# Batch 1 in aligned key sets, one-operation activations for two batches, and other places for the copies of the global values

## The chip, the cores and the metric

The kernel runs on one core of one Trainium2 chip. The metric is the device time of one execution in microseconds. Before the change it is 296.8 us, the median of three runs (296.14 to 297.85).

## The reference, cut to what matters

```python
B, H, Sl, Sg, D = 8, 8, 512, 32, 64          # batches, heads, local and global rows, head size
k_all = concat(k_g, k_l); v_all = concat(v_g, v_l)
out_g = softmax(q_g @ k_all.T / 8) @ v_all   # 32 global rows see all 544 keys
s_ll = q_l @ k_l.T / 8, only where |i - j| <= 32
s_lg = q_l @ k_g.T / 8                       # and all 32 global keys
out_l = softmax(concat(s_lg, s_ll)) @ concat(v_g, v_l)
x = concat(out_g, out_l), heads side by side # 4352 rows of 512
h = x @ w_in                                 # 512 -> 2048
out = (h * sigmoid(1.702 h)) @ w_out         # 2048 -> 512
```

Inputs and output are float32; the kernel multiplies in bf16.

## The kernel before

The work goes batch by batch (i from 0 to 7, and a ninth block of the 256 global rows of all batches). For each there are three kinds of work:

- Attention, in two halves of four heads, `a` and `c` (in each half a head has 32 of the 128 partitions). `Tk` and `Tq` turn keys and queries on VectorE, `ext` puts the global ones beside them, `S(0)` and `S(1)` make the scores on TensorE, `X` the exponentials on ScalarE, `M` multiplies by the mask on VectorE, `U` or `UG` multiplies by the values on TensorE, and `R`, `XL`, `G` or `RXG` divide by the sums on VectorE and write xL (the batch's input of the next stage) and xG (the global rows).
- The hidden stage, `h_mm` and `h_act`: 16 steps of four matmuls of 512 columns, each with tanh on ScalarE and a multiply-add on VectorE (L656), since h * sigmoid(1.702 h) is half of h * (1 + tanh(0.851 h)). The result is `gT`; the half is put into the copy at the end (`o_out`, L687, scale 0.5).
- The output stage, `o_mm`: four blocks of 128 rows (`tci`), each of four groups (`f4`) of four matmuls, then a copy to `ob` on ScalarE and four writes by SP (L698).

The order on every engine is the program's order, written out by hand. The attention of batch i + 1 is laid between the output matmuls of batch i. Below, h0, o0, h1, o1, h2 are the hidden and the output stages of batches 0, 1 and 2. From batch 2 on all batches have one form, class `Wide`: keys in sets of 96 with the 32 global keys beside them (so that one matmul of 128 rows covers both), the values in three copies that start at different keys. `load_v` reads the values and, five times, the global values into `vtiles` (two, used in turn), and `turn_v`, on SP's queue, writes the shifted copies `vturn` in SBUF, in the middle of a hidden stage. Batches 0 and 1 have the older form, class `Quad`: four overlapping windows of keys, global keys apart (`gk`, `K`, `XK`, `ekU`), a shifted copy `ek2` of the global part for half of batch 1 by DMA, and `U` with the values as weights.

PSUM has eight banks of 512 columns: four in two pairs (`spair`, for scores, or for the first four hidden steps of batch 0), and four in the ring `psP` (`pbank`) that hidden, output and value products take in turn. A matmul that starts in a bank waits until the bank's last reader is done. GpSimd issues the loads (each issue also waits for the transfer eight before it) and makes the masks. `after(x)` is a small copy on GpSimd that reads x, and so holds back the loads that stand behind it.

Of the kernel before, what the change touches and what calls it, by code (L numbers as in the profile page):

```python
# [12 lines left out]
F32 = mybir.dt.float32  # L13
# [7 lines left out]
def kernel(  # L21
# [67 lines left out]
    def load_v(b):  # L89
        vt = v_rows(b)  # L90
        if b < 4:
            nc.gpsimd.memset(vt[:, :, :, D:], 1.0)
        vs, vg = (x[b].rearrange("h s d -> s h d") for x in (v_l, v_g))
        for c in range(5):
            nc.gpsimd.dma_start(out=vt[0:96, c, :, :D], in_=vs[96 * c : 96 * c + 96])  # L95
            nc.gpsimd.dma_start(out=vt[96:128, c, :, :D], in_=vg)  # L96
        nc.gpsimd.dma_start(out=vt[0:32, 5, :, :D], in_=vs[480:512])

# [11 lines left out]
    rvg = consts.tile([128, 4, D + 2], BF16)  # L110


    rvt = consts.tile([128, 4, D + 2], BF16)
# [5 lines left out]
    def load_g(lo, hi, names="kqv"):  # L119
        for name, dst, src in (("k", rkg, kgf), ("q", rqg, qgf)):  # L120
            if name in names:
                nc.gpsimd.dma_start(out=dst[:, lo:hi, :], in_=src[:, lo:hi, :])
        if "v" in names:
            load_turned(nc.gpsimd, rvg[:, lo:hi, :D], vgf[:, lo:hi, :])
# [33 lines left out]
    for i in range(2):  # L158
        vtiles.append(consts.tile([128, 8 * 6 * (D + 2)], BF16, name="v%d" % i))
        nc.gpsimd.memset(v_view(i, 4)[:, :, :, :, D:], 1.0)  # L160
# [25 lines left out]
    keep(28, psP.tile([128, 512], F32, name="w", tag="p"), 128)  # L186

    qtiles = []
    for i in range(4):
        qt = consts.tile([128, 24, 32], F32, name="q%d" % i)  # L190
        nc.vector.memset(qt[:, 0:4, :], 0.0)
        nc.vector.memset(qt[:, 20:24, :], 0.0)
        qtiles.append(qt)

    WIN = ((0, 10), (6, 12), (14, 12), (22, 10))
    near_mask = consts.tile([128, 2, LW], BF16)
# [15 lines left out]
    def make_near(c):  # L212
        nr = WIN[c][1]
        at = (0, 160, 0, 192)[c]
        nc.scalar.activation(near_mask[:, c // 2, at : at + 16 * nr].rearrange("p (t r) -> p t r", t=16),
                             near(bandt, c), AF.Copy)

# [5 lines left out]
    def mask_put(g, first, last, by, late):  # L223
# [22 lines left out]
    qgT = consts.tile([128, 4, 40], F32)  # L246
    nc.vector.memset(qgT[:, :, 32:], 0.0)
    kgT = consts.tile([128, 4, 32], F32)
# [12 lines left out]
    def load_rest():  # L261
        load_v2(0)
# [5 lines left out]
        for g4 in (1, 0, 2, 3):  # L268
            nc.gpsimd.dma_start(
                out=w_out_sb[:, 4 * g4 : 4 * g4 + 4, :].rearrange("p (g e) m -> p g (e m)", e=2),  # L270
                in_=w_out_r[:, 2 * g4 : 2 * g4 + 2, :])
            if g4 == 0:
                load(1, (0,))
                load_g(2, 4)
        load(1, (1,))
        load(2, kq=False)
        nc.gpsimd.dma_start(out=loaded[2][1][:, 0], in_=qf[2][:, 0])
        load_g(4, 8, "k")
        load_v2(1)
        load_g(4, 8, "q")  # L280
        nc.gpsimd.dma_start(out=loaded[2][0], in_=kf[2])
        nc.gpsimd.dma_start(out=loaded[2][1][:, 1], in_=qf[2][:, 1])
# [14 lines left out]
    class Quad:  # L297
        def __init__(self, Q):
# [5 lines left out]
            self.v = v_view(self.b, 4 if self.b < 2 else 5)[:, self.u]  # L304
            if self.b < 2:
# [43 lines left out]
        def S(self, rnd, split=False, added=False, part=None):  # L349
# [19 lines left out]
            if not part:  # L369
                self.E[rnd] = att.tile([128, 4, RW + 32], BF16, name="e%d" % rnd)  # L370
# [29 lines left out]
        def M(self, rnd):  # L400
            at = 36 if rnd else 40
            e = self.E[rnd][:, :, at : at + LW]
            nc.vector.tensor_mul(e, e, near_mask[:, rnd : rnd + 1, :].to_broadcast([128, 4, LW]))

# [25 lines left out]
        def XK(self, two=True):  # L430
            self.ek = att.tile([128, Sl], BF16, name="ek")
            nc.scalar.activation(self.ek, self.kb, AF.Exp, scale=scale)
            self.ek2 = None
            if two:
                self.ek2 = att.tile([128, Sl], BF16, name="ek2")
                load_turned(nc.sync, self.ek2, self.ek)

        def ekU(self, unit, warm=0, ov=None):
# [4 lines left out]
            for j in range(4):  # L443
                two = unit == 1 and self.ek2 is not None
                r = 32 * ((j + 1 + two) % 4)
                p = slice(r, r + 32)
                lv = (ones32[p] if unit == 0 else
                      (rvt if two else rvg)[p, self.Q, :D].rearrange("p (w h) -> p w h", h=2)[:, :, unit - 1])
                nc.tensor.matmul(ov[32 * j : 32 * j + 32, :], lhsT=lv, rhs=(self.ek2 if two else self.ek)[p],  # L449
                                 start=True, stop=False, skip_group_check=True)  # L450

        def ekUs(self, nxt=None, rnd=0, banks=(None, None, None)):
# [5 lines left out]
            if self.ek2 is not None:  # L458
                self.ekU(1, ov=banks[1])
            if nxt:  # L460
                nxt.K(1)
            if self.ek2 is None:
                self.ekU(1, ov=banks[1])
# [76 lines left out]
    class Wide(Quad):  # L540
# [9 lines left out]
        def spread(self):  # L550
# [3 lines left out]
            nc.scalar.activation(self.kg4[:, :, 0:96], kl[:, 0:480].rearrange("p (m w) -> p m w", m=5), AF.Copy)  # L554
            nc.scalar.activation(self.kT[:, 640:672], kl[:, 480:512], AF.Copy)
# [15 lines left out]
        def S(self, rnd):  # L571
# [14 lines left out]
            self.E[rnd] = att.tile([128, 4, LW], BF16, name="e%d" % rnd)  # L586
# [13 lines left out]
        def UG(self):  # L600
            self.ov = []
            for lo, hi in self.BANKS:
                ov = pbank("ov")
                self.ov.append(ov)
                work = []
                for t in range(lo, hi):
                    w = min(max(t, 1), 14)
                    work.append((t // 8, t + 1 if t < 8 else t - 8, w, 128, t - lo))
                if hi == 16:
                    work += [(*g, 4) for g in OUTER]  # L610
                for i, (rnd, o, w, n, to) in enumerate(work):
                    rho, m = at_of(w)
# [6 lines left out]
        def RXG(self):  # L619
            rc = att.tile([128, 17, 1], F32, name="rc")  # L620
# [17 lines left out]

    gTs, ops = {}, {}
# [12 lines left out]
    def h_act(i, fc, hp):  # L652
        n = width(i)
        th = moe.tile([128, TB], F32, name="th", bufs=4)
# [23 lines left out]
    def o_out(i, tci, op):  # L678
        ob = moe.tile([128, d_model], F32, name="ob", bufs=6)
        last = i == B and tci == B // 4 - 1  # L680
        for lo, hi in ((0, 320), (320, 512)) if last else ((0, 512),):
# [5 lines left out]
            nc.scalar.activation(ob[:, lo:hi], op[:, lo:hi], AF.Copy, scale=0.5)  # L687
            for j in range(4):
                eng = nc.scalar if last and j % 2 else nc.sync
                if 2 <= i < B:  # L690
# [8 lines left out]

    def act4(i, hf):  # L700
        f = slice(2 * hf, 2 * hf + 2)
        nc.vector.scalar_tensor_tensor(gTs[i][:, f, :], in0=th4s[i][:, f], scalar=1.0, in1=pts[i][hf],
                                       op0=ALU.add, op1=ALU.mult)

    pts, th4s = {}, {}
# [39 lines left out]
    a.XK(False)  # L745
# [5 lines left out]
    c.XK(False)  # L751
# [12 lines left out]
    pt = pts[0] = spair()  # L764
# [17 lines left out]
    th4 = th4s[0] = early  # L782

    def tanh2(hf):
        f = slice(2 * hf, 2 * hf + 2)
        nc.scalar.activation(th4[:, f], pt[hf], AF.Tanh, scale=0.851)

    tanh2(0)
    c.G()
    act4(0, 0)  # L790
    for fc in range(4, FC):
        h_step(0, fc)
        if fc in (5, 6, 8, 9):
            make_near((5, 6, 8, 9).index(fc))
        if fc == 12:
            tanh2(1)
            act4(0, 1)
    load_v(2)
# [7 lines left out]
    load_turned(nc.sync, rvt[:, 2:4], rvg[:, 2:4])  # L806
    nq = {1: (Quad(2), Quad(3)), 2: (Wide(4), Wide(5))}
    a, c = nq[1]
    a.T()
    transpose_g(2, 4)  # L810
    a.ext()
    osteps(0, (0, 1), (0, 0), (1, 1), (1, 0), (2, 1))
    a.S(0)
    a.gg()
    a.K()
    a.X(0)
    a.XK()
    a.M(0)
    a.eg()
    c.T()  # L820
    c.ext()
    osteps(0, (2, 0), (0, 2), (0, 3))
    a.S(1)
    a.X(1)
    a.M(1)
    osteps(0, (1, 2), (1, 3))
    c.S(0)
    c.X(0)
    c.M(0)
    osteps(0, (2, 2), (2, 3))  # L830
    c.S(1)
    a.ekUs(c, 1)
    c.X(1, lambda: c.XK(False))
    for unit in range(3):
        a.U(unit)
    a.R()
    nq[2][0].Tq()
    c.M(1)
    c.eg()
    pt = spair()  # L840
    a.Gm(bank(pt, 0)[:, 0 : D + 2])
    osteps(0, (3, 0), (3, 1))
    a.XL(0)
    a.XL(1)
    c.ekUs(banks=[bank(pt, unit + 1) for unit in range(3)])
    for unit in range(3):
        c.U(unit)
    c.R()
    c.XL(0)
    c.XL(1)  # L850
    a.G()
    c.Gm()
    osteps(0, (3, 2), (3, 3))
    a, c = nq[2]
    gTs[1] = moe.tile([128, FC, TB], BF16, name="gT")

    def loads(i):
        if i + 2 < B:
            after(gTs[i][:, 0])
            load(i + 2)  # L860
            if i == 1:
                load_g(8, NQ, "kq")
            load_v(i + 2)

    hps = [pbank("hp") for _ in range(2)]
    for fc, kcs in ((0, (0, 1)), (1, (0, 1)), (0, (2, 3)), (1, (2, 3))):
        h_mm(1, fc, hps[fc], kcs)
    for fc in range(FC):
        if fc < 2:
            h_act(1, fc, hps[fc])  # L870
        else:
            h_step(1, fc)
        if fc == 0:
            loads(1)
        if fc == 1:
            nq[1][1].G()
        if fc == 2:
            a.Tk()
        if fc == 5:
            a.spread()  # L880
        if fc == 7:
            a.ext()
        if fc == 8:
            turn_v(2)
        if fc == 10:
            a.S(0)
            a.X(0)
    a.M(0)

    def phase_o(i):  # L890
# [11 lines left out]
        if i == 1:  # L902
            c.Tk()
        a.S(1)
        a.X(1)
        if i == 1:
            c.spread()
        a.M(1)
        if i == 1:
            c.Tq()  # L910
            c.ext()
# [97 lines left out]
```

## Time and profile before

| | |
|---|---|
| profiled execution | 297.65 us, of which the span (first to last instruction) is 295.9 |
| median of three runs | 296.8 us |
| TensorE busy | 282.7 us (96%) |
| VectorE, ScalarE, GpSimd busy | 200.7, 161.4, 84.4 us |
| hidden matmuls L648 | 487 recorded, 108.3 us |
| output matmuls L673 | 486 recorded, 119.1 us |
| chain that ended last | PE 86%, DMA 5%, DVE 3%, issue 2%, ACT 2% |

The chain follows the work back from the last instruction, at each step to what released it. "Idle before" is the time in which an engine stood before an instruction, with what ended it. Times in the answers of the trace are microseconds from the start of the span.

### The profile page before, as it was taken

To read this page: it belongs to the slowest core of one execution; us is meant where nothing else is said; L and a number is where in the kernel's file an instruction comes from. 1 tells how busy PE (TensorE), PEld (TensorE's weight loads), DVE (VectorE), ACT (ScalarE), POOL (GpSimd) and SP (SyncE) were. 2 spreads that over 40 slices of the span, in tenths; PEclk is the share of its full clock that TensorE was granted. 3 is DMA by queue.
4 is the path that set the end of the run, shared out by engine and by line. 5 is a ranking of instruction groups with operands and counts; after the bars stand their busy time and mean duration, and the time that the engine had idled before them with its cause. 6 is when DMAs were issued, how large, how long until landed. Compare 5 with 4: busy or idle time off the path is not lost.

```text
span 295.9 us, 9591 instructions
## 1 busy us (share of the span) xinstructions
PE 282.7 (96%) x4076; PEld 145.0 (49%) x4129; DVE 200.7 (68%) x409; ACT 161.4 (55%) x282; POOL 84.4 (29%) x151
## 2 busy tenths in 40 slices
PE   7799999999999999999999999999999999999994
PEld 6354434444554455445454445444544454456553
DVE  6587956997968876777767767787678654773310
ACT  4727567277546645566547734764556551763421
POOL 6853556584504240162107130353000000000000
PEclk9999999999999999999999999999999999999999
DMA  7999999989934992299527992399226012101123
GB/s 196 153 177 210 194 190 212 169 155 210 139 76 115 229 104 67 72 188 193 80 55 153 222 102 55 82 235 151 65 59 181 2 47 65 38 0 35 39 62 80
DMA packets 63418, 35.94 MB, mean 121 GB/s; under 512 B 49808, under 2 KB 52240, under 8 KB 63376
## 3 DMA queue, kind: packets, MB, share of 16 engines
q0 software_dynamic: 53296, 17.77, 56.1%
q1 hardware_dynamic: 9328, 16.85, 20.4%
q10 hardware_dynamic: 752, 0.72, 0.8%
q8 instruction: 32, 0.52, 0.8%
q14 instruction: 10, 0.08, 0.1%
HBM read 36.70 MB, written 8.91 MB: 154 GB/s over the span
## 4 chain that ended last, share of the span: by engine, by line
PE 86%; DMA 5%; DVE 3%; issue 2%; ACT 2%; ACTq 0%; POOL 0%; SPq 0%; DVEq 0%
PE hp L648 38%; PE op L673 35%; PE s L581 5%; PE ov L614 4%; DMA ek<-ek 2%; DMA rk<-in_k_l_dram 2%; PE s L648 1%; ACT e L396 1%; DMA early<-in_k_l_dram 1%; DVE xL L508 1%; PE ov L475 1%; PE op L685 1%; PE s L363 1%; PE ov L449 0%; DVE rs L503 0%
## 5 line engine op out<-in xcount | busy, mean ns | idle before, releaser
L673 PE MATMUL op<-w_out_sb,gT 128*128 128x512 bf16 x486 | 119.1, 380 | 3.5 <-issue 2.1
L656 DVE SCALAR_TENSOR_TENSOR gT<-th,hp 128x512 bf16<-128x512 f32 (+1 forms) x140 | 90.3, 655 | 35.3 <-ACT th L655 34.3
L648 PE MATMUL hp<-xL,w_in_sb 128*128 128x512 bf16 x487 | 108.3, 379 | 0.9 <-DVE xL L508 0.2
L655 ACT ACTIVATE th<-hp 128x512 f32<-128x512 f32 (+1 forms) x140 | 79.1, 572 | 43.2 <-PE hp L648 42.9
L648 PEld LDWEIGHTS <-w_in_sb 128*128 128x128 bf16 x576 | 56.1, 98 | 64.9 <-issue 1.1
L673 PEld LDWEIGHTS <-gT 128*128 128x128 bf16 x528 | 48.3, 98 | 52.4 <-issue 1.4
L590 ACT ACTIVATE e<-s 128x704 bf16<-128x704 f32 x48 | 33.7, 755 | 24.5 <-PE s L581 24.5
L687 ACT ACTIVATE ob<-op 128x512 f32<-128x512 f32 (+2 forms) x35 | 20.5, 585 | 46.2 <-PE op L673 39.8
L596 DVE TENSOR_TENSOR e<-e,mask 128x1024 bf16<-128x1024 bf16 (+1 forms) x24 | 17.4, 724 | 22.4 <-ACT e L590 22.4
L95 POOL DMA_DIRECT2D v<-in_v_l_dram x30 | 23.6, 786 | 23.5 <-PE hp L648 14.1
L96 POOL DMA_DIRECT2D v<-in_v_g_dram x30 | 17.7, 590 | 18.3 <-DMA rk<-in_k_l_dram 14.9
L628 DVE TENSOR_TENSOR xn<-ov,rc 128x384 bf16<-128x384 f32 (+1 forms) x36 | 19.5, 542 | 1.2
L168 POOL CAST tick<-gT 1x1 f32<-1x1 bf16 x5 | 0.9, 174 | 59.8 <-DVE gT L656 59.8
L581 PEld LDWEIGHTS <-kT 32*128 32x128 bf16 x1344 | 12.4, 92 | 10.2 <-issue 9.3
L396 ACT ACTIVATE e<-s 128x856 bf16<-128x856 f32 x14 | 11.7, 881 | 7.3 <-PE s L363 7.3
L581 PE MATMUL s<-q,kT 32*128 32x32 bf16 (+2 forms) x1344 | 15.2, 184 | 0.0
L627 DVE RECIPROCAL rc<-ov 128x6 f32<-128x6 f32 (+1 forms) x36 | 6.6, 183 | 9.8 <-PE ov L614 9.8
L614 PEld LDWEIGHTS <-e 128*32 128x32 bf16 (+1 forms) x1056 | 10.1, 94 | 5.1 <-DVE kl L547 2.1
L547 DVE STREAM_TRANSPOSE kl<-rk 128x512 f32<-128x512 f32 x12 | 12.4, 1034 | 0.1
L560 DVE STREAM_TRANSPOSE q<-rq 128x512 f32<-128x512 f32 x12 | 12.5, 1039 | 0.0
L614 PE MATMUL ov<-v,e 128*32 128x66 bf16 (+1 forms) x528 | 11.0, 197 | 0.0
L614 PE MATMUL ov<-vt,e 128*32 128x66 bf16 x528 | 10.4, 195 | 0.0
(110 smaller groups left out, 187.6 us busy)
## 6 DMA issues: line engine op xcount, KB each, us to landing
out_dram<-ob SPq DMA_DIRECT2D x132, 64.0 KB, 2.0
vt<-v SPq DMA_DIRECT2D x12, 264.0 KB, 8.7
rk<-in_k_l_dram POOLq DMA_DIRECT2D x6, 512.0 KB, 11.7
vt<-v SPq DMA_DIRECT2D x6, 495.0 KB, 5.0
v<-in_v_l_dram POOLq DMA_DIRECT2D x30, 96.0 KB, 9.3
rq<-in_q_l_dram POOLq DMA_DIRECT2D x5, 512.0 KB, 8.3
w_in_sb<-in_moe_w_in_dram POOLq DMA_DIRECT2D x8, 256.0 KB, 9.0
w_out_sb<-in_moe_w_out_dram POOLq DMA_DIRECT2D x4, 512.0 KB, 10.5
```

The lines of the kernel that those rows point to most:

```text
L95: nc.gpsimd.dma_start(out=vt[0:96, c, :, :D], in_=vs[96 * c : 96 * c + 96])
L96: nc.gpsimd.dma_start(out=vt[96:128, c, :, :D], in_=vg)
L581: nc.tensor.matmul(bank(self.ps, j)[:, 0:LW].rearrange("p (t q) -> p t q", q=32)[:, os], lhsT=self.k[p, k0 : k0 + 128, e], rhs=self.q[p, t ...
L590: nc.scalar.activation(self.E[rnd][:, 2 * i : 2 * i + 2, :], self.ps[i][:, :, :LW], AF.Exp, scale=scale)
L596: nc.vector.tensor_mul(e, e, m.to_broadcast([128, 4, n]))
L614: nc.tensor.matmul(ov[32 * j : 32 * j + 32, 66 * to : 66 * to + 66], lhsT=self.E[rnd][0:n, j, 32 * o : 32 * o + 32], rhs=self.vs[rho][0:n, ...
L628: nc.vector.tensor_mul(xn[:, lo // 2 : hi // 2].rearrange("p a h w b -> p a b h w"), o3[:, 0:n, 0:D].rearrange("p (a b) (w h) -> p a b h w ...
L648: nc.tensor.matmul(hp[:, : width(i)], lhsT=w_in_c[:, fc // 4, kc, fc % 4 // 2, :, fc % 2], rhs=(xL[i] if i < B else xG)[:, kc, :], start=( ...
L655: nc.scalar.activation(th[:, :n], hp[:, :n], AF.Tanh, scale=0.851)
L656: nc.vector.scalar_tensor_tensor(gTs[i][:, fc, :n], in0=th[:, :n], scalar=1.0, in1=hp[:, :n], op0=ALU.add, op1=ALU.mult)
L673: nc.tensor.matmul(op, lhsT=gTs[i][:, fc, tci * 128 : tci * 128 + 128], rhs=w_out_sb[:, fc, :], start=(first and fc == 4 * f4), stop=(fc = ...
L687: nc.scalar.activation(ob[:, lo:hi], op[:, lo:hi], AF.Copy, scale=0.5)
```

## The change

Batch 1 gets a form of its own, class `Near`, made from `Wide`: six key sets (the last starts inside the fifth), each multiplied with five blocks of 32 queries, exponentials of two whole banks at once, a mask made on GpSimd (`mask_near`), and values from the one unshifted copy. The hidden steps of batches 0 and 1 use one activation, `Gelu_apprx_sigmoid`, in place of tanh and multiply, and their output is copied with scale 1. `load_v` reads the global values once, and `spread_v` copies them to the other four places on VectorE. `turn_v` moves from the hidden stage to the end of the output stage before it. The order of o0, h1 and o1 is written anew; the second half of `w_out` is loaded later, batch 1 earlier, and batch 2 behind `after(a.rc[:, 0])`. `E`, the scores' buffers, become parts of one tile, `ebuf`. The warm-up matmuls at the start are 20 of 128 rows and 28 of 32 rows, for 28 of 128.

```diff
     def load_v(b):
         vt = v_rows(b)
+        if b == 1:
+            nc.gpsimd.memset(vt[:, 5], 0.0)
...
         for c in range(5):
+            if c == 0:
+                nc.gpsimd.dma_start(out=vt[96:128, c, :, :D], in_=vg)
             nc.gpsimd.dma_start(out=vt[0:96, c, :, :D], in_=vs[96 * c : 96 * c + 96])
-            nc.gpsimd.dma_start(out=vt[96:128, c, :, :D], in_=vg)
         nc.gpsimd.dma_start(out=vt[0:32, 5, :, :D], in_=vs[480:512])
+        if b == 1:
+            nc.gpsimd.dma_start(out=vt[96:128, 5, :, :D], in_=vs[480:512])
+
+    def spread_v(b):
+        vt = v_rows(b)
+        nc.vector.tensor_copy(vt[96:128, 1:5, :, :D], vt[96:128, 0:1, :, :D].to_broadcast([32, 4, 8, D]))
...
+    cold = [psP.tile([128, 512], F32, name="w", tag="p") for _ in range(4)]
+    keep(20, cold[0], 128)
+    for i in range(28):
+        p = slice(32 * (i % 4), 32 * (i % 4) + 32)
+        nc.tensor.matmul(cold[i % 4][:, 0:96], lhsT=warm[p, 0:128], rhs=warm[p, 0:96], start=True, stop=True)
...
-        for g4 in (1, 0, 2, 3):
...
+        w_out(1)
+        load(1, (0,))
+        mask_near()
+        load_g(2, 4)
         load(1, (1,))
-        load(2, kq=False)
...
+        w_out(0)
+        w_out(2)
+        load_v(1)
+        w_out(3)
...
+    NEAR = (
+        ((0, 0, 5, 0), (128, 3, 5, 5), (128, 17, 1, 15), (256, 6, 5, 10)),
+        ((384, 9, 5, 0), (384, 17, 1, 14), (512, 12, 5, 5), (512, 17, 1, 15), (256, 17, 1, 13), (544, 15, 3, 10)),
+    )
+
+    class Near(Wide):
+        def S(self, rnd):
+            self.ps = spair()
+            for k0, lo, n, o in NEAR[rnd]:
+                for e in range(2):
+                    for j in range(4):
+                        p = slice(32 * j, 32 * j + 32)
+                        nc.tensor.matmul(
+                            bank(self.ps, j)[:, 32 * o : 32 * o + 32 * n],
+                            lhsT=self.k[p, k0 : k0 + 128, e], rhs=self.q[p, lo : lo + n, :, e],
...
+        def XM(self, rnd):
+            lo, n, at = ((1, 14, 0), (0, 13, 14))[rnd]
+            m = near_mask[:, at : at + n].rearrange("p (a t) q -> p a (t q)", a=1)
+            for i in range(2):
+                e = self.E[rnd][:, 2 * i : 2 * i + 2]
+                nc.scalar.activation(e, self.ps[i], AF.Exp, scale=scale)
+                e = e[:, :, 32 * lo : 32 * lo + 32 * n]
+                nc.vector.tensor_mul(e, e, m.to_broadcast([128, 2, 32 * n]))
...
     def h_act(i, fc, hp):
         n = width(i)
+        if i < 2:
+            nc.scalar.activation(gTs[i][:, fc, :n], hp[:, :n], AF.Gelu_apprx_sigmoid)
+            return
...
+    osteps(0, (0, 1), (1, 1))
     a.S(0)
+    a.XM(0)
+    c.Tk()
+    c.spread(nc.vector.tensor_copy)
+    c.Tq()
     c.ext()
+    osteps(0, (2, 1), (3, 1), (0, 0))
     a.S(1)
+    a.XM(1)
+    osteps(0, (1, 0), (2, 0), (3, 0))
     c.S(0)
+    c.XM(0)
+    spread_v(1)
+    osteps(0, (0, 2))
     c.S(1)
+    c.XM(1)
+    osteps(0, (1, 2), (2, 2), (3, 2))
+    a.UG(spair())
+    a.RXG()
+    after(a.rc[:, 0])
+    load_v(2)
+    load(2, (0,))
+    load_g(4, 8)
+    load(2, (1,))
+    osteps(0, (0, 3), (1, 3), (2, 3))
+    c.UG()
+    c.RXG()
+    osteps(0, (3, 3))
     a, c = nq[2]
+    spread_v(2)
+    turn_v(2)
+    for x in (a, c):
+        x.Tk()
+        x.spread(nc.vector.tensor_copy)
+        x.Tq()
+        x.ext()
...
+    def phase_o1():
...
+        SXM(a, 0)
+        o(0)
+        o(1, 0, 1)
+        SXM(a, 1)
+        o(1, 2, 3)
+        SXM(c, 0)
+        o(2, 0, 1)
+        a.UG()
+        a.RXG()
+        a2.Tk()
+        o(2, 2)
+        SXM(c, 1)
+        a2.spread()
+        a2.Tq()
+        a2.ext()
+        o(2, 3)
+        o(3, 0, 1)
+        c2.Tk()
+        spread_v(3)
+        c.UG()
+        turn_v(3)
+        c2.spread()
+        c.RXG()
+        o(3, 2)
+        SXM(a2, 0)
+        o(3, 3)
+        c2.Tq()
+        c2.ext()
...
         if n < B:
             c2.Tk()
+            spread_v(n)
         o(2)
         c.UG()
+        if n < B:
+            turn_v(n)
...
-            if fc == 6 and i + 1 < B:
-                turn_v(i + 1)
```

In o1, `a` and `c` are the halves of batch 2, `a2` and `c2` those of batch 3.

## The prediction

> **What bounds the kernel now.** First the page, for the shares.
>
> ```profile
> span 295.9 us, 9591 instructions
> PE 282.7 (96%) x4076; PEld 145.0 (49%) x4129; DVE 200.7 (68%) x409; ACT 161.4 (55%) x282; POOL 84.4 (29%) x151
> ```
>
> TensorE is busy nearly all the time and takes its instructions in program order, so I price the change on its path. The granted clock is 9 in all 40 slices, so the clock is no term. Next, the chain of work that ended last, for where batch 1 loses time.
>
> ```profile
> 41.64 6.70 DMA ek<-ek
> ...
> 57.10 0.39 PE hp L648
> 57.51 0.61 ACT th L655
> 58.14 0.70 DVE gT L656
> 58.88 6.64 PE hp L648 x30
> 65.57 0.38 PE hp L648
> 65.95 0.57 PE s L581 x56
> ...
> 75.06 0.87 PE ov L614 x73
> ...
> 89.41 9.06 PE hp L648 x42
> 98.53 4.70 PE hp L648 x21
> ```
>
> The chain names a 6.70 us transfer of `ek`, which the change removes. But the waits of TensorE up to 92 us put only 0.2 us of waiting on it, the rest lay under output matmuls. At 57 to 59 us TensorE really waits, for tanh and the multiply to free a PSUM bank. From 89.41 on a hidden stage (64 matmuls) takes 13.8 us, 0.2155 each, and a whole batch 121.76 - 89.41 = 32.35 us: 27.6 for 128 matmuls, four `S` of 0.57 and two `UG` of 0.87 (4.02), and 0.73 for six hand-overs, 0.12 each. This is the yardstick. The stretch that the change rewrites runs from 33.86 (output stage of batch 0) to 89.41 (hidden stage of batch 2):
>
> - o0 with batch 1's attention: 33.86 to 55.50, 21.64 us
> - h1, with two `S` of batch 2 inside: 55.50 to 71.50, 16.00
> - o1: 71.50 to 89.41, 17.91
>
> Third, the timelines of VectorE, ScalarE and GpSimd, for prices.
>
> ```profile
> 4.13 0.23 DVE L133 CAST rqg<-g32q 128x128 bf16<-128x128 f32 x1 [0.82 <-DMA g32q<-in_q_g_dram]
> 5.33 0.40 DVE L723 CAST rk<-early 128x512 bf16<-128x512 f32 x1
> 115.17 1.03 DVE L547 STREAM_TRANSPOSE kl<-rk 128x512 f32<-128x512 f32 x1
> 116.94 0.20 DVE L627 RECIPROCAL rc<-ov 128x6 f32<-128x6 f32 x1 [0.74 <-PE ov L614]
> ```
> ```profile
> 2.24 1.28 ACT L714 ACT_TABLE_LOAD   x1 [2.24 <-issue]
> 22.28 1.02 ACT L786 ACTIVATE early<-s 128x1024 f32<-128x1024 f32 x1 [4.73 <-issue]
> 45.37 1.66 ACT L396 ACTIVATE e<-s 128x856 bf16<-128x856 f32 x2 [0.22 <-PE s L363]
> ```
> ```profile
> 29.90 0.70 POOL L269 DMA_DIRECT2D w_out_sb<-in_moe_w_out_dram  x1 [2.02 <-DMA w_out_sb<-in_moe_w_out_dram]
> 32.38 0.70 POOL L269 DMA_DIRECT2D w_out_sb<-in_moe_w_out_dram  x1 [1.78 <-DMA w_out_sb<-in_moe_w_out_dram]
> ```
>
> Between an output stage's last key transpose and its `c.RXG` VectorE has 0.74 us free, and in these stages a block of `w_out` lands every 2.5 us.
>
> **Part 1, batch 1's attention in o0.** The old one fills 21.64 - 13.8 = 7.84 us. The new: two `S` of 32 and two of 48 matmuls, each round 2 x 512 columns per row group. The rows beside it: 56 matmuls over 704 columns take 0.57, the old 16 over 856 take 0.59. Both fit 1.9 ns a matmul plus 0.65 ns a column, so 0.73 and 0.76, 2.98 for four. I take this; the bounds are 0.59 (as the old round) and 1.0. `UG`: 128 matmuls against 88 of the same size in 0.87, so 1.27, 2.54 for two. Hand-overs 0.72. New wait: between `c.S(0)` and `c.S(1)` stand only four output matmuls (0.86), but the two PSUM pairs come free after two exponentials of 1024: the pair of 856 takes 1.66, so 1.94, 2.0 with latencies. TensorE stands 1.1; all other pairs of `S` have 2.6 us of matmuls between. Sum 13.8 + 2.98 + 2.54 + 0.72 + 1.1 = 21.14: **-0.50**.
>
> What feeds it: `a.Tk` to `a.ext` on VectorE are 0.9 + 0.4 + 0.15 + 0.9 + 0.33 = 2.7 us. The first `rk` of batch 1 lands at 34.8 now (issues wait for the transfer eight before; this shows landings); with one `w_out` block (2.5) put behind it, 32.3, the small globals of batch 1 right behind; ready at 35.1, needed at 35.6. That block then lands at 37.6, needed at 38.3. Margins of half a microsecond; lateness costs one for one. The new `near_mask` on GpSimd (one memset of 864, twelve small operations like the mask's 0.12 to 0.37, 4.3 us) stands ahead of the issues that follow, but the queue then holds work until 32 us; without this cover up to 4.3. The values of batch 1 (0.58 MB in 128-byte pieces) follow the third `w_out` block at 40.1 and need some 4 us, wanted at 48.5; `spread_v(1)`, s long, lies between masks that TensorE wants 1.5 us later.
>
> **Part 2, h1.** Less its two `S` (1.38) it took 14.62. One-operation activations free the banks from ScalarE alone, and VectorE has no multiplies to do: 13.86, **-0.76**. The 30 multiplies of batches 0 and 1, some 20 us of VectorE, give nothing else: h0 runs dense already. Four table loads are added, 1.28 each by the row: the first in ScalarE's idle time to 22.3, the second (34.5 to 35.8) before `S` ends at 36.3, the third before 2.6 us of matmuls have filled a pair, the fourth 4 us ahead of the `S` that needs the pair. Cost 0, with gelu priced as the tanh rows (1.02 for 1024, 0.60 for 512). `spread_v(2)`, `turn_v(2)` and both key and query turnings of batch 2 now lie in h1, where VectorE is otherwise idle. [...]
>
> **Part 3, o1.** Before, with the two `S` put here: 17.91 + 1.38 = 19.29. Now `a.UG` begins 40 matmuls and three `S` in, at 8.62 + 2.07 = 10.7. From there VectorE works in this order: first bank 0.37, `a.RXG` 2.88, `a2.Tk` 0.9, mask 0.65, `a2.Tq` 0.88, `ext` 0.33, `c2.Tk` 0.9, then the new `spread_v(3)`, s, and only then `c.RXG`, 2.86 until xL is written: 9.84 + s with the latency. TensorE would be through at 8.04, plus 0.86 for h2's first four matmuls, which need only the first half of xL. So h2 starts in effect at 10.7 + 9.84 + s - 0.86 = 19.68 + s. For s (2048 bf16 on 32 partitions) no row exists: the casts of 128 and 512 (0.23, 0.40) give 0.44 ns an element, so 1.08; bounds 0.4 (the 512 row) and 1.6 (four of them). Part 3: 20.76, **+1.47**. Here the stalls go: queued behind `spread_v(3)` is `c.RXG`, and h2's banks and input wait for that. [...]
>
> **Part 4, later batches and the head.** Each later output stage gets a `spread_v` too: 1.08 against 0.74 free, `c.RXG` 0.3 later, but its result has 2.5 us (written at 119.8, used at 122.6): 0; if s were above 3.2 it would show six times. `turn_v` moves from the middle of a hidden stage to the end of an output stage; on SP its four transfers wait for `spread_v` and for `c.UG`, behind them stand the four writes of the last block, and the ring of six `ob` covers these. They run some 7 us earlier than before (5.0 to 8.7 us to landing by the page), and batch n's `UG` reads them 22 us later: 0. The scores' buffers become parts of one `ebuf`; each part's last reader is a batch back: 0. Fewer copies of the global values relieve a queue nobody waits for. The warm-up is 20 and 28 short matmuls for 28; the first `S` waits for VectorE's q anyway, and ScalarE has 1.1 us before batch 0's third exponential: 0, bounds -0.3 and +0.5.
>
> **Sum.** -0.50 - 0.76 + 1.47 = +0.2. The profiled execution took 297.65 (span 295.9, 1.75 around it) and would take 297.85; it lies 0.85 above the median of 296.8, so the forecast for the median is 297.0: no change. About 0.5%, 1.5 us, is what a measurement here can tell from none.
>
> **Rivals.**
>
> *Batch 2's keys come late (slower).* GpSimd now waits for `a.RXG`'s first reciprocal, at 49.2, before it issues v, q, k and globals of batch 2, where it issued `rk` at 43.2 before; all loads of batch 3 stand behind. `rk` is issued at 55.7. VectorE needs 2.8 us, `S` of batch 2 stands at 68.2: it decides from a landing after 65.4, 9.7 us after the issue. For: the page has 11.7 us as the median of `rk` loads, 12.7 at worst beside `turn_v` at 93 us, and writes and `turn_v(2)` run here too. Against: those are 512 KB, this is 256, and such a one took 8.1 at 34.8. At 12.7: 3.0 us, 300.0. Chance 0.18.
>
> *The weights come late (slower).* If w_out or the values of batch 1 land 2 us later than reckoned, o0 stalls 1.5 to 2: 298.7. For: half a microsecond of margin. Against: the queue's rate is steady, 2.5 a block. Chance 0.12.
>
> *Both new waits are hidden (faster).* If `c.S(1)` does not stand (-1.1) and `spread_v` and `c.RXG` do not reach h2 (-1.5): 294.4. For: yardstick stages have no such wait. Against: the order on VectorE is fixed, and exponentials of 1024 can't end in 0.86. Chance 0.15.
>
> *The forecast* has 0.55; its own range is 295.8 (s at 0.4, `S` at 0.59) to 298.2 (s at 1.6, `S` at 0.85). The whole range, 294.6 to 299.7, leaves out some 2 in 10. Slower by over 0.5%: 0.18 + 0.12 = 0.30; same 0.55; faster 0.15.
>
> **What would show it.** In the changed profile: o0 with attention about 21.1, an idle of 1.1 before one `S` with the exponential as releaser; h1 13.9 with no wait on a multiply; in o1 one wait of about 2 us at h2's first matmuls, on xL or on xn; `spread_v`'s copy at 0.7 to 1.1. Wrong if TensorE waits for a transfer anywhere after 33 us, if h2 starts without a wait, or if a later batch takes other than 32.35.

## The result, and the profile after

The changed kernel takes 298.75 us, median of 17 runs, beside 297.33 for the kernel before: a ratio of 1.0039, 95% interval 1.002 to 1.0057. A second group gave 298.8 beside 296.8, 1.0059 (1.0035 to 1.0082). So it is slower by some 0.5%, about what the prediction called the least that can be told. It had said +0.2 us; measured are +1.4 and +2.0.

The page of the profiled execution, in answer to the lines of before:

```profile
span 297.3 us, 9937 instructions
PE 287.3 (97%) x4309; PEld 145.7 (49%) x4309; DVE 188.2 (63%) x388; ACT 164.1 (55%) x272; POOL 78.5 (26%) x144
PEclk9999999999979999999999999999999999999999
```

VectorE lost 12.5 us of work, as meant. TensorE is busy longer, and its granted clock has one 7, in the slice at 82 to 89 us, where before all were 9. The chain through o1:

```profile
79.48 2.02 issue
...
81.80 1.42 PE op L728 x4
...
85.39 0.76 DVE ebuf L603
...
88.36 0.69 DVE v L106
...
91.33 0.63 DVE xL L641
...
92.00 3.18 PE hp L700 x14
```

The lower half is the chain that the prediction laid out: mask, turnings, `spread_v(3)` (L106), `c.RXG`, xL, h2. The upper half is new: 2.02 us in which TensorE waits for nothing that the profile shows, then four matmuls in 1.42 for 0.86. The waits of TensorE from 33 to 93 us, and the timeline at the place:

```profile
PE ov L621 <- issue: 2.0, 1, 2.0
PE s L659 <- ACT ebuf L673: 0.9, 2, 0.7
PE hp L700 <- DVE xL L641: 0.2, 1, 0.2
```
```profile
81.49 0.28 PE L621 MATMUL ov<-v,ebuf 96*32 96x66 bf16 x12 [2.02 <-issue]
```

The idle lies inside `a.UG` of batch 2, between matmuls of the same line. By windows (length, busy time and count on PE, PEld, DVE, ACT, POOL; then clock, DMA share, GB/s):

```profile
79.50:81.50 2.00, 0.01 (x3) 0.01 (x2) 1.10 (x3) 0.00 (x0) 0.00 (x0) 1.00 1.19 166
83.90:85.30 1.40, 1.40 (x8) 0.53 (x5) 0.48 (x1) 1.34 (x3) 0.00 (x0) 0.50 0.00 0
```

Behind the idle the clock is halved; the trace's clock record gives this 3.413 us (82.18 to 85.59). The half clock does not come in every execution: a stretch of 3.413 us at half speed brings the mean granted clock of 297 us to 0.994, and 11 of the 17 executions have 0.994 or less. Their median is 299.0 us, that of the other six 297.6. In the second group it is 7 of 12, with 299.2 and 298.1. None of the 26 executions of the kernel before in that group lies under 0.997.

Stage by stage, from the starts of TensorE's first instructions (o1 is taken to end 13.90 us before batch 2's next `S`, the length of h2):

| us | o0 | h1 | o1 | sum |
|---|---|---|---|---|
| before (h1 with two `S`) | 21.81 | 15.93 | 17.82 | 55.56 |
| predicted | 21.14 | 13.86 | 20.76 | 55.76 |
| changed | 20.55 | 13.91 | 23.19 | 57.65 |
| changed, another execution | 20.56 | 13.91 | 22.69 | 57.16 |
| changed, without batch 3's values | 20.55 | 13.90 | 20.63 | 55.08 |
| rebuilt, the last experiment | 20.20 | 13.91 | 19.87 | 53.98 |

The three stages lost 2.09 us, o0 started 0.19 earlier, and from o2's first `S` to the end it took 192.20 us for 192.79. That is the whole 1.3 us between the spans. Where the 0.59 behind h2 comes from was not followed up.

### The profile page after: what moved, and what is told of

Its sections match the earlier page's. It is cut to its first block, busy times and chain, and to the rows that moved or that the text cites. A ratio compares the mean times of both kernels' runs of the same rounds, so it can differ in the third digit from the quotient of the medians.

```text
span 297.3 us, 9937 instructions
## 1 busy us (share of the span) xinstructions
PE 287.3 (97%) x4309; PEld 145.7 (49%) x4309; DVE 188.2 (63%) x388; ACT 164.1 (55%) x272; POOL 78.5 (26%) x144
## 4 chain that ended last, share of the span: by engine, by line
PE 90%; DMA 3%; DVE 3%; issue 1%; ACT 1%; ACTq 0%; POOL 0%
PE op L728 39%; PE hp L700 37%; PE s L587 4%; PE ov L621 4%; PE s L700 2%; DMA rk<-in_k_l_dram 2%; DMA early<-in_k_l_dram 1%; PE s L659 1%; PE op L740 1%; PE ov L480 1%; ACT ebuf L414 1%; DVE xn L635 1%; PE s L381 0%; PE s L621 0%; ACT ebuf L673 0%
## 5 line engine op out<-in xcount | busy, mean ns | idle before, releaser
L728 PE MATMUL op<-w_out_sb,gT 128*128 128x512 bf16 x528 | 125.3, 383 | 0.0
L711 DVE SCALAR_TENSOR_TENSOR gT<-th,hp 128x512 bf16<-128x512 f32 (+1 forms) x112 | 71.7, 649 | 30.9 <-ACT th L710 30.4
L710 ACT ACTIVATE th<-hp 128x512 f32<-128x512 f32 (+1 forms) x112 | 62.7, 566 | 36.9 <-PE hp L700 36.7
L597 ACT ACTIVATE ebuf<-s 128x704 bf16<-128x704 f32 x48 | 33.7, 754 | 28.2 <-PE s L587 26.1
L603 DVE TENSOR_TENSOR ebuf<-ebuf,mask 128x1024 bf16<-128x1024 bf16 (+1 forms) x24 | 17.3, 722 | 24.7 <-ACT ebuf L597 24.7
L707 ACT ACTIVATE gT<-hp 128x512 bf16<-128x512 f32 x24 | 14.3, 598 | 5.6 <-PE hp L700 5.5
L621 PEld LDWEIGHTS <-ebuf 128*32 128x32 bf16 (+1 forms) x1312 | 12.5, 94 | 8.1 <-issue 5.9
L621 PE MATMUL ov<-v,ebuf 128*32 128x66 bf16 (+1 forms) x656 | 12.6, 196 | 2.0 <-issue 2.0
L621 PE MATMUL ov<-vt,ebuf 128*32 128x66 bf16 x528 | 10.5, 195 | 0.0
L673 ACT ACTIVATE ebuf<-s 128x1024 bf16<-128x1024 f32 x8 | 7.8, 1021 | 4.0 <-PE s L659 4.0
```

Of the source, the lines that this page charges most:

```text
L597: nc.scalar.activation(self.E[rnd][:, 2 * i : 2 * i + 2, :], self.ps[i][:, :, :LW], AF.Exp, scale=scale)
L603: nc.vector.tensor_mul(e, e, m.to_broadcast([128, 4, n]))
L621: nc.tensor.matmul(ov[32 * j : 32 * j + 32, 66 * to : 66 * to + 66], lhsT=self.E[rnd][0:n, j, 32 * o : 32 * o + 32], rhs=self.vs[rho][0:n, ...
L710: nc.scalar.activation(th[:, :n], hp[:, :n], AF.Tanh, scale=0.851)
L711: nc.vector.scalar_tensor_tensor(gTs[i][:, fc, :n], in0=th[:, :n], scalar=1.0, in1=hp[:, :n], op0=ALU.add, op1=ALU.mult)
L728: nc.tensor.matmul(op, lhsT=gTs[i][:, fc, tci * 128 : tci * 128 + 128], rhs=w_out_sb[:, fc, :], start=(first and fc == 4 * f4), stop=(fc = ...
```

## The experiments

Three theories of the idle: **F**, TensorE waits for its next 16 KB of instructions, held up by transfers (the trace of the changed kernel has 33 packets of 16,384 bytes on its instruction queue, one of them from 79.11 to 80.07 us); **P**, the same, by the density of the program alone; **D**, it waits for data that the trace doesn't show. The kernel before took 297.33, 296.6 and 296.8 in the three groups of runs, so times are compared by their ratio to it.

**1. Without batch 3's values.**

```diff
-            load_v(i + 2)
+            if i > 1:
+                load_v(i + 2)
```

> The values of batch 3 are not loaded (six transfers of small rows on GpSimd's queue are left out, which move from about 65 to 82 us); everything else is as in the changed kernel, and batch 3's output is computed from old values. Theory F (instructions, held up by transfers): the 2.02 us in which TensorE stands inside a.UG of batch 2 with nothing visible to wait for is a wait for its next 16 KB of instructions, whose transfer starts late (79.1 us) because these small rows keep all DMA engines full. Then the idle and the half clock behind it vanish, a.RXG and all of VectorE's chain behind it come 2.0 us (idle) plus 0.6 (slow matmuls before c.S(1)) earlier, and the time is about 296.1. Theory P (instructions, by the density of the program): the block is late because three S and a UG use up 256 instructions in 3 us; the idle stays, 298.7. Theory D (data: a.UG's last group waits for something the trace does not show): the idle stays as well, 298.7.

295.86 us, ratio 0.9964 (0.9939 to 0.9989). The idle is gone, and the half clock with it. From 33 to 93 us TensorE has the 0.9 before `c.S(1)` left, and in the place of the 2.0:

```profile
PE hp L700 <- DVE xL L641: 0.7, 1, 0.7
```

P falls in its plain form, since the order on TensorE is the same. D is not yet out: a transfer of data held up by these loads would come earlier too. o1 takes 20.63, and the prediction had 20.76: without the idle its sum comes out.

**2. All blocks shifted by 128 instructions.**

```diff
-    for i in range(28):
+    for i in range(92):
```

> 64 more short matmuls in the warm-up (92 for 28, some 1.7 us in a stretch where TensorE otherwise stands for the first queries), so that all later instructions of TensorE lie 128 places further on in their 256-instruction blocks; the rest unchanged. Theories F and P: the idle of 2.02 us is tied to the border of a block and not to the instruction, so it leaves its place before the 96-row matmuls of a.UG: it moves by about 128 instructions or is hidden; hidden gives 296.1, moved into the stage's output matmuls 296 to 298.7. Theory D: it stays before the same matmul with the same length, 298.7. If the longer warm-up is not hidden, up to 0.5 comes on top, to be seen at the start of h0 (23.13 us in the changed kernel).

300.21 us, ratio 1.0108 (1.0042 to 1.0174). `a.UG` runs through, and TensorE stands in the `S` behind it:

```profile
83.53 0.50 PE L587 MATMUL s<-q,kT 32*128 32x32 bf16 x44
86.40 0.30 PE L587 MATMUL s<-q,kT 32*128 32x64 bf16 x12 [2.37 <-issue]
```

Counting matmuls and weight loads as recorded, the idle came after row 2496 and now comes after row 2752, exactly 256 later; since 128 were added, that is 128 places further on in the program. So it hangs on a border between blocks of 256, and not on the data of one matmul: D falls. The time got worse for a reason I had not seen: the border at row 704 now lies where the first batch's attention is dense, TensorE stood there 1.65 us, and the clock was at 0.51 from 20.0 to 23.4 us (the profiled execution, 302.18 us, is the slowest of its runs).

**3. Eight matmuls between `c.S(0)` and `c.S(1)`.**

```diff
-    osteps(0, (0, 2))
+    osteps(0, (0, 2), (1, 2))
     c.S(1)
     c.XM(1)
-    osteps(0, (1, 2), (2, 2), (3, 2))
+    osteps(0, (2, 2), (3, 2))
```

> In o0 eight output matmuls for four stand between c.S(0) and c.S(1); the four are taken from behind c.S(1), so nothing is added. Prediction's reason (the PSUM pairs come free after two exponentials of 1024, 1.94 us, and four matmuls cover only 0.86 of it): the idle of 0.2 + 0.67 us before c.S(1) with the exponential as releaser goes, o0 takes 19.7 for 20.55 and the time is 297.9. Rival: the wait only moves to the next scores or to a.UG, which takes the same PSUM pairs: 298.7. The idle inside a.UG of batch 2 should stay under theory D; under F and P it may shift, since its block comes 0.9 us earlier against the transfers.

298.11 us, ratio 1.0051 (1.002 to 1.0081): by time not to be told from the changed kernel. By the trace the idle of 0.87 before `c.S(1)` is gone, and o0 took 20.11 for 20.55. The other half went to `c.S(1)`, which took 1.02 us for 0.70, and to a new idle of 0.28 at a block's border in `a.UG` of batch 1. The idle in batch 2 stayed at its row, 1.65 us.

**4. Tanh and multiply again for batch 1.**

```diff
-        if i < 2:
+        if i < 1:
...
```

Left out above: the output copy of batch 1 halves again, and its first four hidden steps go one by one through `h_act`.

> Batch 1 gets its tanh and multiply back (with the halving at the output copy); batch 0 keeps the one-operation activation. Prediction's part 2: h1 takes 14.62 for 13.91, TensorE waits for VectorE's multiply where the stage begins, and the time is about 299.4 (+0.7), if all of it reaches the end. Rival (the multiply is hidden once no scores stand in h1): h1 stays at 13.9 and the time at 298.7. Second rival: the idle in o1 swallows or moves the difference, since what sets the start of h2 is not TensorE's arrival at o1; then h1 is longer and o1 shorter by the same, 298.7.

314.12 us, ratio 1.0579 (1.054 to 1.0619): none of the expectations. h1 took 32.4 us. VectorE's timeline:

```profile
62.91 1.04 DVE L552 STREAM_TRANSPOSE kl<-rk 128x512 f32<-128x512 f32 x1 [7.27 <-DMA rk<-in_k_l_dram]
...
72.82 0.65 DVE L711 SCALAR_TENSOR_TENSOR gT<-th,s 128x512 bf16<-128x512 f32 x1
```

In the new order the turnings of batch 2, which wait for its keys, stand ahead of h1 on VectorE. With multiplies in h1 these queue behind the keys, and TensorE stands 16.8 us for `gT`. So the new order can't do without the one-operation activation, and the activation's price can't be read from the changed kernel.

The run shows something else as well. While TensorE stands, the values of batch 3 come in; their last transfer lands 5 us before o1 begins. TensorE's order and the borders are those of the changed kernel, the values are loaded, and yet `a.UG` of batch 2 runs through; o1 takes 20.63, as in experiment 1. That is F again, without leaving out any data.

**5. The one-operation activation alone, in the kernel before.**

```diff
+        if i == 1:
+            nc.scalar.activation(gTs[i][:, fc, :n], hp[:, :n], AF.Gelu_apprx_sigmoid)
+            return
...
```

> The kernel before with one part of the change alone: batch 1's hidden stage uses the one-operation activation in place of tanh and multiply (and its output copy does not halve). Prediction's part 2: TensorE no longer waits for tanh and multiply at 57 to 59 us; the stage with its two S takes 15.2 for 16.0 and the time falls by 0.7 to 0.8 against the kernel before (296.6 for 297.3). Rival (the two S of batch 2 with their exponentials lie in the middle of this stage, so ScalarE has to load its table twice more, 1.28 each, and the banks come free that much later): the gain is eaten, 297.3 to 298.5.

298.53 us, ratio 1.0072 (1.0055 to 1.009): slower, the rival. ScalarE's timeline around the first `S` inside h1:

```profile
65.56 1.28 ACT L590 ACT_TABLE_LOAD   x1
66.85 1.41 ACT L590 ACTIVATE e<-s 128x704 bf16<-128x704 f32 x2
68.28 1.28 ACT L655 ACT_TABLE_LOAD   x1
```

From the last hidden activation (to 65.51) to the next (69.57) 4 us pass in which no bank of h1 comes free; TensorE waits 1.20 for it, and h1 with its two `S` takes 17.04 for 15.93. That is 1.1 us of the 1.9 between the medians. In the profiled execution o0, which the edit does not touch, takes 22.49 for 21.81, with a wait of 0.92 for queries where the kernel before had 0.16; so not all of the 0.7% need be the activation's.

**6. TensorE's order evened out, and the borders moved.**

```diff
-    for i in range(28):
...
+    keep(2, cold[1], 512)
...
-        o(0)
-        o(1, 0, 1)
+        o(0, 0, 1, 2)
         SXM(a, 1)
-        o(1, 2, 3)
+        o(0, 3)
+        o(1, 0, 1)
         SXM(c, 0)
-        o(2, 0, 1)
+        o(1, 2, 3)
+        o(2, 0)
         a.UG()
...
-        o(2, 2)
+        o(2, 1, 2, 3)
         SXM(c, 1)
...
-        o(2, 3)
```

> The changed kernel with TensorE's order in o1 evened out: 12 output matmuls between any two of S, S, S and a.UG (for 24, 8 and 8), 12 behind a.UG and 8 behind the next S (for 4 and 12); and 2 matmuls of 512 columns in the warm-up for 28 of 96, which is about the same time and moves all borders of 256 instructions back by 52 places. VectorE's order as in the changed kernel. Theory F with the density (the block is late because transfers hold its fetch up to 2.8 us, lands 1 us later, is used 1.4 us later, and the 256 instructions before it last only 3.0 us): the same block now lasts about 5.9 us, so the idle of 2.02 and the half clock go; then h2 waits for VectorE's chain as in the run without batch 3's values and the time is 296.2. Theory that the fetch is simply late at this time of the run, whatever is executed: the idle stays about 2 us, 298.7.

296.74 us, ratio 1.0011 (0.9994 to 1.0027), and the idle is gone. Now h2 waits for VectorE, as the prediction had it:

```profile
PE hp L698 <- DVE xL L639: 0.7, 1, 0.7
PE hp L698 <- DVE xn L633: 0.6, 1, 0.6
```

**7. The same with VectorE's order changed.**

```diff
+        a2.Tk()
         a.UG()
         a.RXG()
-        a2.Tk()
...
-        SXM(c, 1)
         a2.spread()
         a2.Tq()
         a2.ext()
+        SXM(c, 1)
...
-        spread_v(3)
         c.UG()
-        turn_v(3)
...
         o(3, 3)
+        spread_v(3)
+        turn_v(3)
```

> As the evened kernel, and VectorE's order in o1 changed: a2.Tk ahead of a.UG's results, a2.Tq and ext ahead of the mask of c.S(1), and spread_v(3) and its turn_v(3) behind c.RXG and the mask of a2.S(0). Prediction's part 3 (h2's start is set by VectorE's chain, in which spread_v(3), 0.69 us, and the turnings stand ahead of c.RXG): h2's wait for xL falls from about 1.2 us to 0.4 or less and the time is 1 to 1.5 below the evened kernel, about 295.0. Rival (TensorE and not VectorE sets it): no difference between the two. A third way: spread_v and the turnings of c2, now later, stand ahead of h2's first multiplies, and TensorE waits there what it gained before.

296.35 us, ratio 0.9989 (0.9968 to 1.0009). The waits on xL and xn are gone, o1 takes 20.84 for 21.50. The third way took part of it: 0.68 us before `c.UG` for the mask of `c.S(1)`, and 0.5 in h2 for a multiply behind the turnings.

**8. The same with the edit of experiment 3.**

> As the kernel with VectorE's order changed, and eight output matmuls for four between c.S(0) and c.S(1) in o0. If the parts add up (0.4 to 0.9 us by the run with that edit alone, the borders of the blocks being others here): about 294.4, faster than both the kernel before and the changed one. If the block that TensorE then needs in a.UG of batch 1 comes late, as it did by 0.28 us in that run, half of it is lost: 294.8.

295.86 us, ratio 0.9968 (0.9943 to 0.9993), and not the 294.4 to 294.8 expected. o0 takes 20.23 for 20.55, with an idle of 0.35 at a border, in its `c.UG` this time: of the 0.87 gained before `c.S(1)` 0.32 is left. The profiled execution, the longest of its ten, also has 0.8 us of waiting for `turn_v(3)` at 107 us, which experiment 7 had put late.

**9. The changed kernel once more.**

> The changed kernel unchanged, as the yardstick of this group. If the idle in a.UG of batch 2 belongs to the program and its transfers, the profile shows it again at the same matmul (before the 96-row ones), 1.5 to 2.5 us long, with or without 3.4 us of half clock behind it; 298.7 by the first time, 298.0 against the level of the kernel before in the later groups. If it was an accident of one execution, it is not there.

298.8 us, ratio 1.0059 (1.0035 to 1.0082). The idle is at the same matmul:

```profile
80.02 0.28 PE L621 MATMUL ov<-v,ebuf 96*32 96x66 bf16 x12 [2.15 <-issue]
```

This execution had no half clock behind it, and o1 took 22.69 for 23.19. Against 20.63 without the idle, the idle costs 2.06 and the half clock 0.5; the rest of the slow stretch is taken from h2's wait for VectorE, 0.7 us here and 0.2 there. In this execution o0 started at 31.89 us, in the first at 33.50: a head of the same code varies more than the 0.19 of the first comparison.

**10. `spread_v(3)` early, in the kernel of experiment 6.**

```diff
         SXM(a, 1)
+        spread_v(3)
...
-        spread_v(3)
         c.UG()
```

> The kernel with o1 evened out, with one edit: spread_v(3) stands behind the mask of a.S(1), where VectorE has some 2.4 us free, and no longer ahead of c.RXG. Prediction's part 3: the copy's own 0.69 us leaves the chain to h2's start; the waits of h2's first matmuls fall from 0.56 + 0.73 us to about 0.6 in all, the time by 0.7 (296.0 for 296.7). Rival (TensorE is there no earlier, or c.UG sets the chain): nothing changes.

296.38 us, ratio 0.9972 (0.9952 to 0.9992), against 1.0011 with the copy in its old place. One wait of h2 is left:

```profile
PE hp L698 <- DVE xL L639: 0.5, 1, 0.5
```

h2's waits fall from 1.3 to 0.5 us, o1 from 21.50 to 20.55. The copy was on the path, for at least its own 0.69 us.

**11. The evened order with the borders where they were.**

> The kernel with o1 evened out, but with the 28 short matmuls of the warm-up back, so that the borders of 256 instructions lie where the changed kernel has them. By the count of instructions the block that was late now begins 21 rows into c.S(0) and lasts 3.8 us (0.5 of S, 2.6 of output matmuls, 0.7 of a.UG); by the changed kernel's own numbers a block is in use 5.2 us after its predecessor begins (2.83 to the start of the transfer, 0.96 of transfer, 1.42 until it is used). So TensorE should stand about 1.4 us again, after some 140 of the 176 rows of a.UG (matmuls and weight loads): 297.4 to 298.1. Rival (the evened order alone cured it, borders do not matter): no idle, 296.7.

299.3 us, ratio 1.0074 (1.0048 to 1.01):

```profile
81.52 0.24 PE L621 MATMUL ov<-v,ebuf 96*32 96x66 bf16 x8 [2.47 <-issue]
```

The place was foretold nearly (76 of the 88 matmuls are through, some 152 rows for 140), the length was not: 2.47 for 1.4. The rival falls: the order alone cures nothing. The single packets of the instruction queue (16,384 bytes each) show why. For the block concerned, with every 256th recorded row (704, 2496 and so on) as a border:

| us | border before it | packet starts | lands | needed | runs on |
|---|---|---|---|---|---|
| changed | 76.29 | 79.11 | 80.07 | 79.5 | 81.49 |
| changed, again | 74.68 | 77.66 | 78.61 | 77.9 | 80.02 |
| shifted by 128 | 81.67 | 84.02 | 84.94 | 84.0 | 86.40 |
| eight between (3) | 76.38 | 79.02 | 79.96 | 79.6 | 81.22 |
| evened, old borders | 75.10 | 79.18 | 80.12 | 79.1 | 81.52 |
| evened, borders moved | 73.98 | 77.87 | 78.76 | 80.6 | no idle |
| without batch 3's values | 75.70 | 76.22 | 77.18 | 78.7 | no idle |
| tanh for batch 1 (4) | 94.26 | 95.04 | 95.98 | 97.2 | no idle |
| before | 75.67 | 76.62 | 78.22 | 80.5 | no idle |

In all five with the idle TensorE runs on 1.26 to 1.46 us after the packet has landed. The packet starts 0.5 us after the border without the values, 0.8 where they had landed before, 2.4 to 4.1 where they are on their way. I had taken 2.83 for a constant. It isn't one, but the place is: in the five runs of the table with these loads in o1 whose border lies 6.8 to 8.3 us after o1's start, the packet starts 10.9 to 11.3 us after it. So the loads set its time, and not the border. What in them holds it is not simply that the DMA engines are full: they are full in the kernel before too (9 in all 40 slices from 75.6 to 76.7 us), where it took 0.95. This stays open. In the kernel before the blocks of that stretch last 4.6 to 6.6 us, in the changed one this block (one `S`, eight output matmuls and most of a `UG`) lasts 3.0. So in these runs a late packet does harm where the block is dense, and none where the block lasts longer.

**12. The parts together.** Experiment 6, the edit of 3, `spread_v(3)` as in 10, and:

```diff
+        a2.Tk()
         a.UG()
         a.RXG()
-        a2.Tk()
-        o(2, 1, 2, 3)
-        SXM(c, 1)
+        o(2, 1, 2)
         a2.spread()
         a2.Tq()
         a2.ext()
+        SXM(c, 1)
+        o(2, 3)
         o(3, 0, 1)
...
-        c2.Tq()
-        c2.ext()
...
+            if i == 2 and fc == 2:
+                nq[3][1].Tq()
+            if i == 2 and fc == 6:
+                nq[3][1].ext()
```

> What the runs point to, together: o1 evened out, the borders moved, eight output matmuls between c.S(0) and c.S(1) in o0, spread_v(3) in VectorE's free time behind the mask of a.S(1), a2's queries ahead of the mask of c.S(1), twelve matmuls between c.S(1) and c.UG so that this mask is done in time (0.68 us of idle in the run before), and c2's query turnings inside h2 behind its third activation (0.52 us of idle ahead of h2's fifth bank). If these idles go and nothing takes their place: 1.0 to 1.2 below the best so far, about 294.8 against 296.6 for the kernel before. If the multiplies of h2 then wait for the turnings in h2 itself, 0.5 of it is lost.

294.93 us, ratio 0.9942 (0.9913 to 0.9971), faster than both kernels. From 33 to 93 us the profile lists two waits of TensorE, 0.3 and 0.2 us, both put down to "issue"; those on the exponential, the mask, xL, xn and `gT` are gone.

## Why the prediction was right or wrong, point by point

The forecast, no change within 0.5%, came out at the edge of that bound (0.39% and 0.59%), and that it did is luck, by errors that offset each other: o0 was 0.59 us better than forecast, the rest behind h2 0.59, and o1 2.43 worse. The forecast's own range reached to +1.4 us, which the first group just meets and the second, at +2.0, passes. (That range does not quite follow from its terms: they give 295.7 to 297.9, for 295.8 to 298.2.) The chance of 0.30 for slower stood on late keys and late weights, and neither happened.

- **Part 1, o0: 21.14 forecast, 20.55 measured.** The stall before `c.S(1)` was there, 0.87 for 1.1, with the exponential as releaser and 1.94 us for two of 1024, as worked out. The mis-sized term is `S`: the fit of 1.9 ns a matmul and 0.65 ns a column gave 2.98 for four, and they take 0.59, 0.64, 0.60 and 0.64, 2.47. The lower bound, "as the old round", was the nearer row. `UG` was 1.18 and 1.27 for twice 1.27. These three terms make 0.83; hand-overs took 0.24 more than reckoned. The margins of half a microsecond on keys and weights held here; in experiment 6 the first `S` waited 0.3 for its keys.
- **Part 2, h1: 13.86 forecast, 13.91 measured.** The number is right, the reason half wrong. With the one-operation activation alone (experiment 5) h1 gets slower. And of the 0.76 that the prediction put down to tanh and multiply, 0.52 is a wait for xL: from the first hidden matmul to the sixth pass 1.60 us for 1.08, with tanh (55.50 to 57.10) and without (54.70 to 56.30). The rows of the sixth, of the kernel before and of experiment 5:

```profile
57.10 8.85 PE L648 MATMUL hp<-xL,w_in_sb 128*128 128x512 bf16 x38 [0.22 <-DVE xL L508]
56.30 8.58 PE L648 MATMUL hp<-xL,w_in_sb 128*128 128x512 bf16 x38 [0.22 <-DVE xL L508]
```

  Tanh and multiply made up 0.27: the 38 matmuls took 8.85 us with them and 8.58 without. The changed kernel gains since xL is early, no `S` stands in h1 and VectorE has no multiplies; how much each of the three gives was not taken apart.
- **The table loads cost nothing, as forecast.** Three of the four, 1.28 us each (from 17.44, 34.32 and 54.87), fall where ScalarE waits anyway, as this one does:

```profile
34.32 1.28 ACT L673 ACT_TABLE_LOAD   x1
36.02 1.94 ACT L673 ACTIVATE ebuf<-s 128x1024 bf16<-128x1024 f32 x2 [0.42 <-PE s L659]
```

  The fourth (68.68 to 69.96) holds back the first exponential of batch 2, but 24 output matmuls stand before the next `S`. Where ScalarE doesn't wait (experiment 5) a load is 1.28 and the next activation starts 0.01 later.
- **Part 3, o1: 20.76 forecast, 23.19 measured.** This is the step that failed, not by its chain, which the runs bear out (20.63 without the idle, and less with `spread_v(3)` out of it), but by what it left out: TensorE's supply of instructions, at nothing in the sum and 2.06 us in the trace, and the half clock behind it, at nothing ("the clock is no term") and 0.5. s was 0.69, not 1.08: the price worked out from the casts of 128 and 512 was too high. The lower end of the 0.7 to 1.1 foretold for the copy is where it came out, though no run before the change shows such a copy. That the sum still comes within 0.13 of 20.63 is in part luck: with s 0.39 too dear, the other terms of the chain were some 0.25 too cheap (from the start of `a.UG` to xL written 10.78 us, for 10.92 reckoned). The wait of 2 us at h2 shrank to 0.2, since TensorE came late itself; with the idle gone it is 0.7 to 1.3.
- **"Wrong if TensorE waits for a transfer anywhere after 33 us"**: it did, for one that the profile does not name. The kernel before has the same wait once, outside the stretch that the prediction looked at, 0.36 us at the border near row 704:

```profile
23.18 0.21 PE L493 MATMUL og<-rvg,eg 128*32 128x66 bf16 x3 [0.36 <-issue]
```

  Its packet had landed at 21.84, 1.34 us earlier, as in the five runs above. The packets of the instruction queue were there to be counted, too, and the block of one `S`, eight output matmuls and most of a `UG` stood in the new order.
- **Part 4.** The later batches take 32.28 to 32.32 us for 32.35, as forecast; `spread_v` and `turn_v` are hidden there.
- **The rivals.** Batch 2's keys were issued at 54.99 and landed by 63.59, before the 65.4 from which they would have decided. No weights came late. The loss had another mechanism than any rival; that 298.75 is nearly the 298.7 of the rival on weights is chance.

## What to carry to other kernels

When a change makes a program denser in small instructions, count them: 256 matmuls and weight loads in 3 us (3.8 in experiment 11) were more than the refill could follow while the loads of a batch ran. An idle that the profile calls "issue" in the middle of one group, always at the same count, is told from a data wait by shifting the program a known number of instructions (256 recorded rows later for 128 added, in experiment 2). And a cheaper operation is worth what its place allows: the one-operation activation made its stage 1.1 us longer in the old order, and the new order did not work without it.

## What the runs showed of the hardware that I had not expected

- TensorE's instructions come in packets of 16,384 bytes: 32 in the kernel before for 8205 recorded matmuls and weight loads, 33 in the changed one for 8618, and in experiment 2 the idle moved by exactly 256 such rows. In the five runs of the table with the idle a block is in use 1.26 to 1.46 us after its packet landed, where TensorE waits for it. The wait was 1.65 to 2.47 us in one place.
- An idle of 2.02 us was followed by 3.413 us at half clock, and one of 1.65 in experiment 2 by 3.4 (0.51 from 20.0 to 23.4 us); idles of 2.15, 2.37 and 2.47, and one of 1.65 in experiment 3, were not. So the length of an idle alone does not decide: experiment 11, with the longest, has no granted clock under 0.998 in eight executions. In the clock records of the kernels before and after, every state but the last, which the end cuts off, lasts a whole number of 3.413 us, within 0.03: 85 before, and 22, 1 and 62 after. The half clock set in 0.69 us after TensorE ran on, at 82.18 us. What decides whether it comes was not shown.
